# A delta-rule attention and a top-1 router on one core: another order for the attention pipeline, and list scatters that don't wait for each other

## The chip, the cores and the metric

One core of a Trainium2 chip. The time is that of one execution on the device, in microseconds (us). Three runs of the kernel before are known, with a median of 893.73 us (889.64 to 895.54).

## The reference

Two blocks follow each other, all in float32.

```
# attention: 4 batches x 8 heads, 768 tokens, head size 48
k_n = k / (|k| + 1e-6)
for t in range(768):
    y[t]   = q[t] @ state                       # state: 48 x 48 per batch and head, zero at first
    v_old  = k_n[t] @ state
    state += beta[t] * outer(k_n[t], v[t] - v_old)
# the heads side by side: x has 3072 tokens of 384
# router: 8 experts, top 1
logits = (x / |x|) @ (emb / |emb|).T / tau
e      = argmax(logits);  gate = softmax(logits)[e]
out    = gate * (relu(x @ w1[e]) @ w2[e])       # w1: 384 x 1024, w2: 1024 x 384 per expert
```

## The kernel before, in words

**Attention.** Tokens are taken in 12 chunks of 64; a pair of batches stands on the two halves of the 128 partitions (`P2` = 2 such pairs, index `p`; `g` is the half). In a chunk the recurrence is solved in closed form with the inverse of a 64x64 triangular matrix per batch and head. The matrices come from `products` (keys against keys and queries, line 259, masked by `later` on VectorE, line 263). Their 32x32 diagonal blocks for two chunks (a pair `s`) travel through memory: `blocks_out` writes them, `blocks_in` reads them with one block on each partition, `weigh` (GpSimd, line 282) multiplies by beta, `eliminate` (VectorE, lines 290 and 292) inverts them in 31 steps of two operations, `inverses_back` sends them to memory and back, `turn` transposes them, and `lower1` and `lower2` (lines 316 and 326) make the full inverse `W`.

For chunk `c`, `residual` takes the state's part from the values (line 337, subtraction on VectorE in line 348), `solve` applies `W` (line 357), `update` and `keep` bring the state forward with `kl` (unit keys made once more on GpSimd, line 237, from a second load of the keys, `Kl`), and `outputs` makes the chunk's result. `store` writes it to memory as `x`; `turned` and `logits` (line 419) make the router's logits with the transposed tokens as weights and 8 columns. `route` runs after every fourth chunk, three times: it finds the expert and gate of 512 tokens, counts their places (a prefix over 8 columns of tokens, lines 470 and 471) and scatters token numbers into the list `idmap` with eight transfers (line 482).

The order is written out by hand in one loop over `c` from -6 to 11. Iteration `c` works on chunk `c`, makes `W` for `c+1` (`cl`), transposes and products for `c+5` (`cf`), key norms and unit keys for `c+6` (`cn`), and some elimination steps in between (`steps(n)`) and operations of `route` (`fill(n)`). Each engine and each queue takes its instructions in this order. All loads, `Kl` among them, are issued by SyncE; `blocks_out` stands behind the loads of K, Kl and V of the same iteration. All scatters are issued by GpSimd, which waits for one to land before it issues the next.

**Experts.** When all tokens are listed, the lists are cut into 31 tiles of 128 tokens of one expert. For each tile SyncE reads its list (line 632) and both weight matrices (lines 638 and 640), GpSimd gathers the tokens, TensorE transposes them and does both products (lines 654 and 659), and GpSimd scatters the result.

Of the kernel before, what the change touches and what calls it, by code (L numbers as in the profile page):

```python
# [15 lines left out]
C = 64  # L16
# [5 lines left out]
def kernel(  # L22
# [11 lines left out]
):  # L34

# [60 lines left out]
    for g in range(2):  # L96
        nc.gpsimd.iota(tokid[64 * g:64 * g + 64], pattern=[[C, NC], [2 * S, P2]], base=g * S, channel_multiplier=1)
    run = cpool.tile([128, E], F32, name="run")
# [12 lines left out]
    for i in range(P2):  # L111
        Qs.append(ac.tile([128, NP, 2, 64], F32, name=f"Qp{i}"))
        nc.gpsimd.memset(Qs[i], 0.0)
        KNs.append(ac.tile([128, NP, 2, 64], F32, name=f"KN{i}"))
        nc.gpsimd.memset(KNs[i], 0.0)

    def heads(t):

        return t.rearrange("p (a b) d -> p b a d", a=2)

    def load(src, c, name, bufs):
        ts = []
        for p in range(P2):
            t = wk.tile([128, H, D], F32, name=name, tag=name, bufs=bufs)
            for g in range(2):
                nc.sync.dma_start(out=t[64 * g:64 * g + 64],
                                  in_=src[2 * p + g, :, c * C:(c + 1) * C, :].rearrange("h t d -> t h d"))
            ts.append(t)
        return ts

    def load_q(c):
        for p in range(P2):
            for g in range(2):
                for hh in range(2):
                    nc.sync.dma_start(out=Qs[p][64 * g:64 * g + 64, :, hh, 0:D],
                                      in_=q[2 * p + g, hh * NP:(hh + 1) * NP, c * C:(c + 1) * C, :]
                                      .rearrange("h t d -> t h d"))
# [3 lines left out]
    Kf = {0: load(k, 0, "K", 4)}  # L141
    load_q(0)
    Kf[1] = load(k, 1, "K", 4)
# [10 lines left out]


    rtau = ac.tile([128, 1], F32, name="rtau")
    nc.scalar.dma_start(out=rtau, in_=moe_tau.broadcast_to([128, 1]))
    nc.vector.reciprocal(rtau, rtau)
    enT = ac.tile([128, KC, E], F32, name="enT")
    emb = wk.tile([128, Dm], F32, name="emb", tag="R")[0:E]  # L160
    nc.scalar.dma_start(out=emb, in_=moe_expert_emb)
    esq = wk.tile([128, Dm], F32, name="esq", tag="R")[0:E]
    ess = ac.tile([E, 1], F32, name="ess")
    nc.scalar.activation(esq, emb, ACT.Square, accum_out=ess)
    nc.gpsimd.tensor_tensor(out=ess, in0=ess, in1=half[0:E, 0:1], op=ALU.pow)
    nc.vector.tensor_scalar_add(ess, ess, 1e-6)
    nc.vector.reciprocal(ess, ess)
    nc.vector.tensor_scalar_mul(esq, emb, ess)
    psE = bank("f", 3)[:, 0:KC * E].rearrange("p (a e) -> p a e", e=E)
    for j in range(KC):  # L170
        nc.tensor.transpose(psE[:, j, :], esq[:, j * 128:(j + 1) * 128], ident[0:E, 0:E])
    nc.vector.tensor_copy(enT, psE)


    none = ac.tile([128, NMAP // 128], I32, name="none")
    nc.gpsimd.iota(none, pattern=[[0, NMAP // 128]], base=N, channel_multiplier=0)
    nc.scalar.dma_start(idmap.rearrange("(p n) o -> p (n o)", p=128), none)
    zrow = ac.tile([1, Dm + 1], F32, name="zrow")
    nc.vector.memset(zrow, 0.0)
    nc.scalar.dma_start(x_dram[N:N + 1, :], zrow)  # L180
# [17 lines left out]
    for i in range(4):  # L198
        Sb.append(ac.tile([128, 2, NP, 2, D], F32, name=f"S{i}"))
        nc.gpsimd.memset(Sb[i], 0.0)  # L200
# [3 lines left out]
    rns, KQs, APs, kls, Ws, Bks, Tks, Tds, Wds, xcs, Zs = ({} for _ in range(11))  # L204
# [3 lines left out]
    def squares(c):  # L208
# [3 lines left out]
        for p in range(P2):  # L212
            Ksq = wk.tile([128, H, D], F32, name="Ksq", tag="Ksq")
            nc.gpsimd.tensor_tensor(Ksq, Kf[c][p], Kf[c][p], op=ALU.mult)
# [488 lines left out]
```

## Time and profile before

| | |
|---|---|
| median of three runs | 893.73 us |
| the profiled execution | 899.38 us, of which the span of instructions is 897.7 us |
| granted TensorE clock, mean of the span | 0.809 of full speed |
| TensorE products busy | 640.2 us (71% of the span) |
| VectorE, ScalarE, GpSimd busy | 268.5, 158.7 and 212.8 us |

The profile is that of one execution. A granted clock of 1.00 is 2.4 GHz, 0.50 is 1.2 GHz; there are these two levels, and a mean lies between them. A line's number is that of the kernel above. The busy time of an engine says little by itself: TensorE's in the experts' part is not changed by what the attention does. What sets the time of a stretch is the wait that ends last in it.

### The profile page before, as it was taken

The numbers are of one execution on the slowest core, as the hardware profiler recorded it, in microseconds if no ns is written. First come the engines' busy times: TensorE is split into PE (matmuls) and PEld (weight loads), VectorE is DVE, ScalarE is ACT, GpSimd is POOL, SyncE is SP. The second block draws the span as 40 slices with busy tenths as digits, with TensorE's granted clock in tenths as the row PEclk, the third lists the DMA queues.
The fourth block names the chain that finished last, engine by engine and source line by source line (L and its number), as shares of the span: only waits on it lengthen the run. The fifth ranks groups of instructions, "written<-read, shape, count | busy, mean of one in ns | idle before, by whom it ended". The sixth has DMA issues, their size and how long they took to land.

```text
span 897.7 us, 18377 instructions
## 1 busy us (share of the span) xinstructions
PE 640.2 (71%) x7748; PEld 543.3 (61%) x7748; DVE 268.5 (30%) x713; ACT 158.7 (18%) x316; POOL 212.8 (24%) x214
## 2 busy tenths in 40 slices
PE   0525373895829059979763019999999999999995
PEld 0424373894828048878763017777777777777773
DVE  2419674672843036783004000000000000000000
ACT  0211041342312013432321001111111111111110
POOL 4734433223320241110221211211211111111110
PEclk9955577786665557965777559999999999999998
DMA  3343747536443014533030059999999999999930
GB/s 63 67 87 60 137 88 151 88 73 134 89 83 67 8 33 80 116 77 67 2 73 18 0 209 383 380 311 306 324 296 332 300 318 319 301 316 312 312 124 0
DMA packets 216020, 146.00 MB, mean 163 GB/s; under 512 B 164890, under 2 KB 199873, under 8 KB 215938
## 3 DMA queue, kind: packets, MB, share of 16 engines
q1 hardware_dynamic: 210000, 133.75, 52.8%
q0 software_dynamic: 4736, 10.85, 4.0%
q8 instruction: 61, 1.00, 0.5%
q10 hardware_dynamic: 1202, 0.23, 0.1%
q14 instruction: 21, 0.17, 0.1%
HBM read 128.92 MB, written 17.25 MB: 163 GB/s over the span
## 4 chain that ended last, share of the span: by engine, by line
PE 50%; issue 16%; DVE 14%; DMA 12%; POOL 5%; SPq 1%; ACT 1%; POOLq 0%; DVEq 0%
PE psH L654 17%; PE psO L659 16%; DMA idmap<-tokid,slot_i 9%; DVE tmp L290 4%; DVE Tk L292 3%; PE f L326 3%; PE f L246 3%; PE r L357 2%; DVE AP L263 2%; PE f L419 2%; PE r L337 2%; PE f L259 1%; DVE xTm L648 1%; PE f L316 1%; DMA Kl<-in_k_dram 1%
## 5 line engine op out<-in xcount | busy, mean ns | idle before, releaser
L654 PEld LDWEIGHTS psH<-xTm,w 128*128 128x128 f32 x1488 | 170.9, 193 | 18.7 <-DVE xTm L648 14.5
L654 PE MATMUL psH<-xTm,w 128*128 128x128 f32 x1488 | 174.4, 277 | 10.8 <-DVE xTm L648 10.3
L659 PE MATMUL psO<-w,hT 128*128 128x384 f32 x496 | 165.1, 486 | 0.0
L659 PEld LDWEIGHTS psO<-w,hT 128*128 128x128 f32 x496 | 91.9, 190 | 57.5
L661 DVE TENSOR_SCALAR y<-psO,xg 128x384 f32<-128x384 f32 x31 | 19.2, 618 | 319.9 <-PE psO L659 319.9
L656 ACT ACTIVATE hT<-psH 128x512 f32<-128x512 f32 x62 | 37.0, 597 | 363.2 <-PE psH L654 306.3
L290 DVE TENSOR_TENSOR tmp<-Bk,Tk 128x31 f32<-128x31 f32 (+15 forms) x186 | 74.5, 401 | 7.4 <-POOL Bk L282 2.5
L357 PE MATMUL r<-R,W 64*64 64x48 f32 x704 | 30.5, 251 | 60.6 <-DVE R L348 60.4
L634 POOL DMA_INDIRECT xg<-x_dram,ids x31 | 30.1, 971 | 183.1 <-DMA ids<-idmap 109.8
L292 DVE TENSOR_TENSOR Tk<-Tk,tmp 128x31 f32<-128x31 f32 (+15 forms) x186 | 68.5, 368 | 6.4
L357 PEld LDWEIGHTS r<-R,W 64*64 64x64 f32 x704 | 28.3, 167 | 64.6 <-DVE R L348 60.5
L662 POOL DMA_INDIRECT out_dram<-y,ids x31 | 31.3, 1009 | 124.0 <-DVE y L661 121.2
L259 PE MATMUL f<-KQ 48*64 48x128 f32 x768 | 37.1, 325 | 32.0 <-DVE AP L263 32.0
L482 POOL DMA_INDIRECT idmap<-tokid,slot_i x24 | 23.5, 978 | 136.8 <-DMA idmap<-tokid,slot_i 76.2
L259 PEld LDWEIGHTS f<-KQ 48*64 48x64 f32 x768 | 29.9, 165 | 35.5 <-DVE AP L263 33.4
L337 PE MATMUL r<-S,KQ 128*64 128x96 f32 x704 | 48.5, 302 | 0.7 <-issue 0.7
L647 PE MATMUL psX<-ident,xg 128*128 128x128 f32 x93 | 13.5, 278 | 49.4 <-DMA xg<-x_dram,ids 49.4
L326 PE MATMUL f<-Wd,PI 64*64 64x32 f32 x768 | 36.6, 264 | 16.6 <-ACT PI L318 16.5
L326 PEld LDWEIGHTS f<-Wd,PI 64*64 64x64 f32 x768 | 35.1, 189 | 19.6 <-ACT PI L318 18.9
L647 PEld LDWEIGHTS psX<-ident,xg 128*128 128x128 f32 x93 | 11.4, 143 | 54.9 <-issue 52.6
L247 ACT ACTIVATE KQ<-f 128x512 f32<-128x512 f32 x48 | 28.3, 597 | 90.8 <-PE f L246 90.3
L337 PEld LDWEIGHTS r<-S,KQ 128*64 128x64 f32 x704 | 41.0, 174 | 3.2 <-issue 1.9
(123 smaller groups left out, 653.1 us busy)
## 6 DMA issues: line engine op xcount, KB each, us to landing
w<-in_moe_w_dram SPq DMA_DIRECT2D x62, 1536.0 KB
K<-in_k_dram SPq DMA_DIRECT2D x48, 96.0 KB
Qp<-in_q_dram SPq DMA_DIRECT2D x96, 48.0 KB
Kl<-in_k_dram SPq DMA_DIRECT2D x48, 96.0 KB
V<-in_v_dram SPq DMA_DIRECT2D x48, 96.0 KB
x_dram<-xc SPq DMA_DIRECT2D x24, 192.0 KB
a_dram<-AP SPq DMA_DIRECT2D x48, 64.0 KB
Bk<-a_dram SPq DMA_DIRECT2D x6, 512.0 KB
```

The costliest lines, as they stand in the source:

```text
L247: nc.scalar.activation(KQs[c, p][:, :, :, i, :], psT.rearrange("p a (g t) -> p a g t", g=2), ACT.Copy)
L259: nc.tensor.matmul(psG[hh][64 * g:64 * g + 64, 128 * hp:128 * hp + 128], lhsT=KQ[r, hp, g, 0, :], rhs=KQ[r, hp, g, :, :], start=True, stop ...
L290: nc.vector.tensor_tensor(tv, Bk[:, i, i + 1:Q].unsqueeze(2).broadcast_to(sh), Tk[:, i:i + 1, 0:i + 1].broadcast_to(sh), op=ALU.mult)
L292: nc.vector.tensor_tensor(Tk[:, i + 1:Q, 0:i + 1], Tk[:, i + 1:Q, 0:i + 1], tv, op=ALU.subtract)
L326: nc.tensor.matmul(psW[r, m, :], lhsT=PI[r, m, :], rhs=Wds[s][r, n + m, :], start=True, stop=True, skip_group_check=True)
L337: nc.tensor.matmul(ps1[64 * g:64 * g + 64, 2 * D * hp:2 * D * (hp + 1)], lhsT=KQs[c, p][:, hp, g, i, :], rhs=state(c, p)[:, g, hp].rearran ...
L357: nc.tensor.matmul(psZ[r, h, :], lhsT=Ws[c][r, p * H + h, :], rhs=R[r, h, :], start=True, stop=True, skip_group_check=True)
L634: nc.gpsimd.indirect_dma_start(out=x, out_offset=None, in_=x_dram[:, :], in_offset=bass.IndirectOffsetOnAxis(ap=ids[:, 0:1], axis=0))
L654: nc.tensor.matmul(psH[:, i], lhsT=w1[:, j, (f + i) * 128:(f + i + 1) * 128], rhs=xT[:, j, :], start=(j == 0), stop=(j == KC - 1))
L656: nc.scalar.activation(hT[:, f:f + 4, :], psH, ACT.Relu)
L659: nc.tensor.matmul(psO, lhsT=hT[:, f, :], rhs=w2[:, f, :], start=(f == 0), stop=(f == NF - 1))
L662: put = nc.gpsimd.indirect_dma_start(out=out[:, :], out_offset=bass.IndirectOffsetOnAxis(ap=ids[:, 0:1], axis=0), in_=y, in_offset=None, b ...
```

## The change

- **Own prologue.** The loop starts at -5. Ahead of it, the norms and unit keys of chunks 0 and 1 are made with VectorE in GpSimd's place, chunk 0 is transposed, and the router's embeddings, the fill of the list and the zero row move into a function `embeddings` that is called behind this. The first zero fills go from GpSimd to VectorE, and the keys of chunk 1 are loaded on ScalarE's queue.
- **Early products.** In an iteration the two `products` stand between residuals, solves and update, and `blocks_out` right behind them. Key products are masked by VectorE as before; query products are copied by ScalarE and masked by GpSimd (`causal`), in tiles of their own.
- **Late transposes.** Those of chunk `c+6` stand at the end of iteration `c`, between `lower1`, `outputs`, `turned` and `lower2`, which are cut into halves by batch pair.
- **Four array quarters.** `residuals` has 48x64 weights for each head in place of 96 wide pairs of heads (twice as many products), and the outputs of the second pair change halves of the partitions. The `f` accumulators get four banks, `r` two.
- **Transposed logits.** The embeddings, padded to 32, become the weights; the result is copied and transposed back, one iteration later.
- **Spread transfers.** A chunk's queries come in four transfers in place of eight; Q, K and V are issued at the start of an iteration, `Kl` by ScalarE's queue behind `keep`.
- **Unchained scatters.** The eight scatters of a round are declared independent, with a one-element fill between them; each list read waits for all scatters. The prefix over tokens is done by nine products, not by sixteen operations.

```diff
-    Kf = {0: load(k, 0, "K", 4)}
+    Kf = {0: load(k, 0, "K", 4), 1: load(k, 1, "K", 4, nc.scalar)}
     load_q(0)
-    Kf[1] = load(k, 1, "K", 4)
...
+            nc.vector.tensor_tensor(As[c][:, p, hh:H:2], G[:, :, 0], later.broadcast_to([128, NP, C]), op=ALU.mult)
+            nc.scalar.activation(Ps[c][:, p, hh:H:2], G[:, :, 1], ACT.Copy)
+
+    def causal(c, p):
+        nc.gpsimd.tensor_tensor(Ps[c][:, p], Ps[c][:, p], later.broadcast_to([128, H, C]), op=ALU.mult)
...
+    def residuals(c):
         if c == 0:
+            return Vl[c]
+        psK = [bank("r", 2), bank("r", 2)]
+        for p in range(P2):
+            for hp in range(NP):
+                for g in range(2):
+                    for hh in range(2):
+                        r = slice(64 * hh, 64 * hh + D)
+                        o = (p * NP + hp) * D
+                        nc.tensor.matmul(psK[hh][64 * g:64 * g + 64, o:o + D], lhsT=KQs[c, p][r, hp, g, 0, :],
+                                         rhs=state(c, p)[r, g, hp, hh, :], start=True, stop=True,
...
     def logits(c, xTs):
+        psL = bank("f", 4)
+        for i in range(KC):
+            for p in range(P2):
+                nc.tensor.matmul(psL[Q * p:Q * p + Q, 0:128], lhsT=enT[:, i, :], rhs=xTs[p][:, i, :],
+                                 start=(i == 0), stop=(i == KC - 1), skip_group_check=True)
+        lT = wk.tile([P2 * Q, 128], F32, name="lT", tag="lT", bufs=1)
+        nc.scalar.activation(lT, psL[0:P2 * Q, 0:128], ACT.Copy)
...
-        for i, w in enumerate((mask_su, ones)):
-            nc.tensor.matmul(psR[:, i], lhsT=w, rhs=ohf, start=True, stop=True, skip_group_check=True)
+        for j in range(J):
+            nc.tensor.matmul(psR[:, (j + 1) * E:], lhsT=ones, rhs=ohf[:, 0:(J - j) * E],
+                             start=(j == 0), stop=False, skip_group_check=True)
+        nc.tensor.matmul(psR[:, 0:J * E], lhsT=mask_su, rhs=ohf, start=False, stop=True, skip_group_check=True)
...
         for j in range(J):
-            nc.gpsimd.indirect_dma_start(
+            put = nc.gpsimd.indirect_dma_start(
                 out=idmap[:, :], out_offset=bass.IndirectOffsetOnAxis(ap=slot_i[:, j:j + 1], axis=0),
+                in_=tokid[:, b * RC + j // P2, j % P2:j % P2 + 1], in_offset=None).ins
+            tc.declare_no_dep(put, group="places", reason="each token has a place of its own")
+            tc.add_to_no_dep_group("places", put)
+            puts.append(put)
+            nc.gpsimd.memset(between, 0.0)
...
-    for c in range(-6, NC):
+    for c in range(2):
+        sq = squares(c, nc.vector)
+        for p in both:
+            sums(c, p, sq)
+        root(c)
+    inverse_norms(0)
+    unit_keys(0, nc.vector)
+    for p in both:
+        for i in range(2):
+            transposes(0, p, i)
+    load_q(1)
+    Kf[2] = load(k, 2, "K", 4)
+    inverse_norms(1)
+    unit_keys(1, nc.vector)
+    embeddings()
+    for c in range(-5, NC + 1):
```

One iteration after the change, with the conditions at its ends left out (`back` is the pair whose inverses come back, in odd iterations):

```
inverses_back(back); load_q(cn); load K(cn+1); load V(cl)          # SyncE
Rs = residuals(c); squares(cn), sums(cn, 0); unit_keys_again(c, 0..1)
products(cf, 0); solve(c, 0); sums(cn, 1); root(cn); logits(c - 1); solve(c, 1); steps(1)
products(cf, 1); blocks_out(cf); by_token_again(c - 1)
update(c, 0..1); keep(c, 0..1); load Kl(cl)                         # Kl: ScalarE's queue
steps(2); inverse_norms(cn); unit_keys(cn); causal(cf, 0..1)
if cf is odd: blocks_in, diagonal, weigh
steps(4); fill(5); outputs(c, 0); turn(back); transposes(cn, 0, 0); lower1(cl, 0)
steps(2); fill(3); outputs(c, 1); transposes(cn, 0, 1); known(cl); lower1(cl, 1)
steps(2); fill(3); turned(c, 0); store(c); transposes(cn, 1, 0); lower2(cl, 0)
turned(c, 1); transposes(cn, 1, 1); lower2(cl, 1); squared(c, 0..1)
steps(4 if odd else 20); fill(4)
```

## Rows read from the trace of the kernel before

**Rows 1.** The page's chain of waits, by line: shares of the span.

```profile
PE psH L654 17%; PE psO L659 16%; DMA idmap<-tokid,slot_i 9%; DVE tmp L290 4%; DVE Tk L292 3%; PE f L326 3%; PE f L246 3%; PE r L357 2%; DVE AP L263 2%; PE f L419 2%; PE r L337 2%; PE f L259 1%; DVE xTm L648 1%; PE f L316 1%; DMA Kl<-in_k_dram 1%
```

**Rows 2.** Stretches: start, chunk loop, experts (columns: length, busy us, granted clock, DMA).

```profile
core 0: us, PE busy (x) PEld busy (x) DVE busy (x) ACT busy (x) POOL busy (x), PEclk, DMA share, GB/s
0.00:123.80 123.80, 45.49 (x545) 39.23 (x545) 65.77 (x162) 16.93 (x28) 58.80 (x65) 0.70 0.47 87
123.80:479.50 355.70, 250.68 (x5125) 231.46 (x5124) 158.92 (x435) 104.55 (x225) 83.17 (x79) 0.71 0.38 74
...
524.30:897.70 373.40, 342.97 (x2077) 271.66 (x2077) 33.65 (x62) 37.01 (x62) 61.38 (x62) 0.97 0.86 291
```

**Rows 3.** Stretches: two chunks in a row, a slow chunk, the one behind it.

```profile
155.40:215.50 60.10, 46.58 (x964) 43.05 (x964) 35.06 (x86) 20.00 (x42) 19.32 (x18) 0.76 0.52 101
325.20:354.20 29.00, 26.81 (x483) 24.67 (x484) 20.06 (x50) 9.46 (x20) 7.98 (x8) 0.68 0.44 83
354.20:371.30 17.10, 17.06 (x471) 15.70 (x470) 11.06 (x31) 8.87 (x19) 0.00 (x0) 1.00 0.26 59
```

**Rows 4.** Timeline of TensorE in the last two of those stretches.

```profile
348.53 2.83 PE L337 MATMUL r<-S,KQ 128*64 128x96 f32 x32
...
355.26 0.66 PE L246 MATMUL f<-ident,Qp 128*128 128x128 f32 x4
...
356.81 1.06 PE L259 MATMUL f<-KQ 48*64 48x128 f32 x30
...
368.28 1.50 PE L419 MATMUL f<-enT,xT 128*128 128x8 f32 x12
369.72 1.54 PE L337 MATMUL r<-S,KQ 128*64 128x96 f32 x32
```

**Rows 5.** Line 482 by itself: time from a scatter's issue to its landing.

```profile
DMA to landing us min/median/max: 3.0/4.0/4.9
```

**Rows 6.** Timeline of GpSimd: scatters of two rounds (start, us, idle before).

```profile
287.80 1.21 POOL L482 DMA_INDIRECT idmap<-tokid,slot_i  x1 [20.96 <-DVE slot_i L479]
...
322.55 1.61 POOL L214 TENSOR_TENSOR Ksq<-K 128x384 f32<-128x384 f32 x2
...
489.94 1.06 POOL L482 DMA_INDIRECT idmap<-tokid,slot_i  x1 [8.74 <-DVE ends L610]
```

**Rows 7.** Timeline: K's loads and the blocks on SyncE's queue, line 282.

```profile
193.53 2.66 SPq L126 DMA_DIRECT2D K<-in_k_dram  x4
...
202.85 2.20 SPq L271 DMA_DIRECT2D a_dram<-AP  x4
...
210.50 2.34 POOL L282 TENSOR_TENSOR Bk<-Bk,bb 128x1024 f32<-128x1024 f32 x1 [15.00 <-DMA Bk<-a_dram]
```

**Rows 8.** Groups by line (count, busy us, mean ns, idle before).

```profile
L290 DVE TENSOR_TENSOR tmp<-Bk,Tk 128x31 f32<-128x31 f32 (+15 forms) x186 | 74.5, 401 | 7.4 <-POOL Bk L282 2.5
L263 DVE TENSOR_TENSOR AP<-f,later 128x512 f32<-128x512 f32 x48 | 30.3, 673 | 32.0 <-PE f L259 32.0
L292 DVE TENSOR_TENSOR Tk<-Tk,tmp 128x31 f32<-128x31 f32 (+15 forms) x186 | 68.5, 368 | 6.4
L282 POOL TENSOR_TENSOR Bk<-Bk,bb 128x1024 f32<-128x1024 f32 x6 | 14.0, 2339 | 90.9 <-DMA Bk<-a_dram 90.9
```

**Rows 9.** Timeline of the tail: the first two prefix operations of the last round.

```profile
485.08 0.17 DVE L470 TENSOR_TENSOR rk<-rk,run 128x8 f32<-128x8 f32 x1
485.28 0.17 DVE L471 TENSOR_TENSOR run<-run,rk 128x8 f32<-128x8 f32 x1
```

**Rows 10.** Timeline of the start: first transposes, first elimination step, first solve.

```profile
28.78 1.11 PE L246 MATMUL f<-ident,KN 128*128 128x128 f32 x4 [7.65 <-POOL KN L229]
...
64.07 0.18 DVE L290 TENSOR_TENSOR tmp<-Bk,Tk 128x31 f32<-128x31 f32 x1
...
123.78 1.87 PE L357 MATMUL r<-V,W 64*64 64x48 f32 x32
```

**Rows 11.** Timeline of VectorE: the same shape beside GpSimd, and alone.

```profile
166.69 0.96 DVE L290 TENSOR_TENSOR tmp<-Bk,Tk 128x175 f32<-128x175 f32 x1
...
195.76 0.34 DVE L290 TENSOR_TENSOR tmp<-Bk,Tk 128x175 f32<-128x175 f32 x1
```

More of the change, by code (lines that the diff above doesn't have):

```diff
@@ L365, in update @@
                 for hh in range(2):
[L366 removed]
+                    h = 2 * hp + hh
                     r = slice(64 * g, 64 * g + 64)
@@ L525 @@
-        if has(c):
-            Rs = [residual(c, p) for p in both]
+        back = (c + 1) // 2 if odd and 0 <= (c + 1) // 2 < NS else None
+        if back is not None:
+            inverses_back(back)
+        if cn >= 2 and has(cn):
+            load_q(cn)
+        if has(cn + 1) and cn + 1 > 2:
+            Kf[cn + 1] = load(k, cn + 1, "K", 4)
+        if has(cl) and c >= -1:
+            Vl[cl] = load(v, cl, "V", 4)
+        if odd and 0 <= (c + 3) // 2 < NS:
+            elim = eliminate((c + 3) // 2)
@@ L527 @@
+        if has(c):
+            Rs = residuals(c)
+        if cn >= 2 and has(cn):
+            sq = squares(cn)
+            sums(cn, 0, sq)
+        if has(c):
+            for p in both:
+                unit_keys_again(c, p)
         if has(cf):
-            transposes(cf, 0, 0)
-            transposes(cf, 0, 1)
-            transposes(cf, 1, 0)
-        steps(3)
+            products(cf, 0)
         if has(c):
             solve(c, 0, Rs[0])
-        if has(cf):
-            transposes(cf, 1, 1)
+        if cn >= 2 and has(cn):
+            sums(cn, 1, sq)
+            root(cn)
@@ L536 @@
+        if has(c - 1):
+            Lp = logits(c - 1, xTs)
         if has(c):
             solve(c, 1, Rs[1])
+        steps(1)
         if has(cf):
[L539 to L548 removed]
+            products(cf, 1)
+            blocks_out(cf)
@@ L549 @@
+        if has(c - 1):
+            by_token_again(c - 1, *Lp)
+            if (c - 1) % RC == RC - 1:
+                behind.append(route((c - 1) // RC))
         if has(c) and c < NC - 1:
@@ L580 @@
                 squared(c, p)
-            logits(c, xTs)
-            fill(20)
-            if c % RC == RC - 1:
-                behind.append(route(c // RC))
+        steps(4 if odd else 20)
+        fill(4)
     fill(1000)
@@ L632, in fetch @@
         got = nc.sync.dma_start(ids, idmap[bass.ds(s, T), :]).ins
+        for put in puts:
+            tc.add_manual_dep(got, put.name, mybir.DependencyInfo(mybir.DependencyClass.Sync, mybir.DependencyReason.DATA),
+                              reason="all tokens are in their places")
         x = mk.tile([128, Dm + 1], F32, name="xg", tag="xg", bufs=4)
```

323 lines of the change are left out of this document (157 added, 166 removed).

## The prediction

> **What bounds the kernel now.** I read the chain of waits first, then the stretches, then the queues. In the chain the experts' products (lines 654 and 659) hold a third of the span, and the list scatters of line 482 a further 9% [rows 1]: 24 transfers of 128 numbers each, which no engine computes. The stretches cut the span into four [rows 2]: a start of 123.8 us to the first chunk's solve, a chunk loop of 355.7 us (12 chunks, 29.6 us each), a routing tail of 44.8 us between that row's end and the next row's begin, and the experts' 373.4 us with TensorE 92% busy at a granted clock of 0.97. The change leaves the experts' code alone apart from a wait ahead of the first list read, so all is decided in the first 524.3 us. There TensorE is busy for 250.7 us of the loop at clock 0.71, and that clock is the second thing to see. A stretch whose granted clock is 1.00 (2.4 GHz) holds 471 matrix products in 17.1 us with TensorE never idle; the one just before it, nearly as full with 483, took 29.0 us at 0.68 [rows 3]. One line's 32 products took 1.54 us in the one and 2.83 us in the other [rows 4]. So a loop stall costs its length and then slow products behind it. The queues say where the stalls come from. GpSimd issues eight scatters per routing round, each waiting for the one before to land, 3.0 to 4.9 us [rows 5]; in the first round it is held from 287.8 until line 214 at 322.55 [rows 6], and TensorE with it. GpSimd also sits 15 us before line 282, six times and 90.9 us in all [rows 7, 8]: the 32x32 blocks leave only when SyncE has issued K, Kl and V loads, from 193.5 to 202.85, and come back at 210.5.
>
> **Scatters.** The wait between scatters goes. A scatter's instruction is 0.96 to 1.2 us long [rows 6], the added one-element fill is short; I take 1.07 us per scatter, 8 x 1.07 + 4.0 for the last landing = 12.5 us in place of 34.3 us (489.94 to 524.3). If the queue takes them no faster than one landing, nothing is gained; if the issue costs nothing, 30 us is. I take 12.5, since 0.96 us is what the instruction itself shows. In the two earlier rounds GpSimd is held 8.6 us instead of 35, and the next chunk's keys (line 237) and squares stand behind it. The list read now waits for all 24 scatters; behind it on SyncE wait the first two tiles' weights, as before.
>
> **Rest of the tail.** Sixteen prefix operations (0.17 us each, 0.20 from start to start [rows 9]) become two: -3.0 us. Eighteen products with 128-column weights stand in for four: at 0.125 to 0.23 us each (line 419, 12 in 1.50 us [rows 4], and nearly double that when slow) this is +1.7 to +3.2 us, I take 2. The transposed logits add a copy, a transpose and a copy, +1 us. So the 10.4 us from the last logits to the first scatter stay. Tail 10.4 + 12.5 = 22.9, against 44.8: **-21.9**.
>
> **Start.** The first transposes stood at 28.78 us, the first elimination step at 64.07, the first solve at 123.78 [rows 10]. The own prologue squares on VectorE, splits the first K loads over two queues, drops one iteration and moves the router's embeddings behind the first transposes. I put the transposes at 17 us. The embeddings then stand ahead of chunk 0's products on TensorE (transposes), ScalarE and VectorE, and eat some of it: elimination at 48.5, that is -15.5. From there to the solve 59.7 us become 51.5, of which the 31 steps themselves are 31 x (0.401 + 0.368) = 23.8 us [rows 8] and stay. First solve at 100: **-24**. Bounds: -8, if the embeddings' transfers hold everything, and -33.
>
> **A full chunk.** The warm stretch is a whole chunk but for 12 of its 16 transposes: 17.1 + 12 x 0.165 = 19.1 us of TensorE [rows 3, 4]. "Four quarters" turns 32 residual products of 0.048 us into 64 of some 0.035 us (line 259, which has four quarters already: 30 in 1.06): +0.7. The logits with 32 weight columns drop from 1.50 us to about 0.6. TensorE floor: 18.9 us, if its clock stays up. VectorE: 35.1 us busy in a pair of chunks [rows 3]; line 263's eight passes of 0.673 us become eight of half the size (0.34 to 0.67; I take 0.36), so 32.5, or 16.3 us per chunk, with issue gaps of 0.03 us some 17.7. Here GpSimd matters. A multiply of line 290 on 175 elements took 0.34 us by itself and 0.96 us while GpSimd worked [rows 11]. The change adds two masks per chunk there, 2 x 1.17 us by half of line 282's 2.34 us [rows 8]. I add 2 to 3 us: VectorE 20 us. The two engines wait for each other at the residuals (behind the last elimination steps of the chunk before), at the new keys and at the turn of the inverses; I give 3.5 us: **23.5 us** per full chunk, bounds 19.5 and 30 (the present pair's 60.1 / 2).
>
> The Trainium skill's page "SBUF — State Buffer", section "SBUF: two separate sides", calls the port pair of VectorE and GpSimd "an exclusive lock, not a bandwidth split", which speaks against the added masks. The trace agrees as to sign, 0.96 against 0.34 us; what it would make of the time is a rival below.
>
> **What covers the rest.** The blocks now leave after the early products with three, not four, groups of loads ahead of them, and those issued at the chunk's start; line 282's result is needed a chunk later, so its wait lies beside TensorE's outputs and transposes. If that cover fails, 15 us per pair come back. Kl's four issues move to ScalarE, 2.66 us by SyncE's row for four [rows 7], where the output evictions queue behind them, and so do four half-size copies of query products per chunk (1.4 to 2.7 us by line 263's 0.673); ScalarE has 105 us of work in 356 [rows 2], 8.7 per chunk, so both cost nothing unless a chunk runs under 15 us. The late transposes fill the gap in which TensorE waited for the inverses. What is late next is VectorE.
>
> The page "DMA: Bandwidth & Descriptors", section "Rules for kernel authors", of the Trainium skill holds that spreading transfers over queues "only saves sequencer issue time". Here that time is what stands ahead of the blocks, so by the rule, too, the 9 us of issue are worth having, and no landing gets shorter.
>
> **Light chunks.** From the eighth on, products and transposes are gone: 17.1 - 64 x 0.035 - 0.7 = 14 us of TensorE, and the two residual and solve round trips have less beside them. I take 19, 18, 17, 16 and 12 us, 82 in all. The routing rounds add 13: in the first, the power of line 429 queues behind line 282 on GpSimd and VectorE waits for it (about 6), and both rounds hold the next keys 3 to 4 us. Loop: 7 x 23.5 + 82 + 13 = 259.5 us: **-96**.
>
> **Sum.** 100 + 259.5 + 22.9 + 373.4 = 755.8 us of span, and 1.7 us around it: 757.5 us against the profiled 899.38. That execution lies 5.6 us above the median of 893.73, so I take as much off: **752 us**.
>
> **Rivals.** *VectorE or a slow clock keeps the old pace* (18%): the stalls go, but full chunks run at 29 us and light ones at 19.5, since waits for VectorE let the clock fall as at 325 us. Loop 7 x 29 + 97.5 + 13 = 313.5, time 806. For: the present pair keeps 29 to 30 us even in the chunk without the 15 us wait, with TensorE 92% busy at 0.68. Against: its idle part was the turn, which now has transposes beside it.
> *VectorE stands still while GpSimd computes* (12%): three pairs of key operations of 1.6 us each [rows 6], two masks of 1.17 and half of line 282, 8.4 us per chunk, come on top of 17.7: full chunks of 26.1 us, 770. That is the rule of "SBUF — State Buffer" in the Trainium skill taken whole. For: the 0.96 us. Against: VectorE's mean of 0.40 us on line 290 has such meetings in it [rows 8].
> *All fits* (8%): full chunks of 20, light ones of 14.5: loop 225, time 718. For: the 17.1 us stretch. Against: VectorE's 20 us.
> *The scatters stay chained* (4%), by the queue itself or an order kept elsewhere: 22 us at the end and some 26 in the loop return: 800. For: no two scatters overlap in the trace. Against: the wait shown is for the landing.
> *Slower* (2%): kl and the square root for the same chunk stand on GpSimd behind line 282 and the scatters. If each chunk waits w for it, and the clock stays at 1.2 GHz, TensorE's work is 1.84 times as long (2.83 / 1.54): 7 x 34.8 + 5 x 25.8 = 373 us, plus 12w. Start and tail give 45.9, so it decides from w = 3.1 us on (373 + 12w > 355.7 + 45.9 + 9); with 8 us it is 961. Against: GpSimd's own work, 83 us in the loop [rows 2], leaves it half idle even with the masks.
>
> **Numbers.** The forecast has 56% and by itself spans 725 to 782 (full chunk 20.5 to 26, start -12 to -30). With the lock, the chained case and most of the old-pace case, and a little of the fast one, 722 to 812 leaves out about 2 in 10. About 1% is what a measurement can tell from no change; faster by more than that: 0.96, within: 0.02, slower: 0.02.
>
> **What would show it.** Line 482's eight scatters 1.0 to 1.1 us apart; no TensorE idle of over 3 us in the loop; first solve near 100 us; stretches of full chunks at clock 0.9 or more and 22 to 25 us long; the wait of line 282 still there, but no TensorE wait behind it. It is wrong if VectorE waits long for GpSimd's keys or masks, or if the experts' stretch is not 373 us.

## The result, and the profile after

The changed kernel takes 832.23 us (median of four runs, 829.93 to 833.08) against 893.29 us for the kernel before on the same chip: a ratio of 0.9316, 95% interval 0.9279 to 0.9353. Forecast were 752 us, with a range of 722 to 812. The sign was right; of 141 us of gain 61 came. The profiled execution took 832.31 us (span 830.6), so it lies on its median; the 5.6 us taken off in the forecast's last step have no counterpart here.

Here are the stretches of the changed kernel (columns as in [rows 2]): start, chunk loop, tail, experts.

```profile
0.00:109.60 109.60, 44.81 (x579) 40.44 (x581) 73.65 (x175) 25.04 (x52) 58.04 (x59) 0.67 0.49 92
109.60:419.70 310.10, 236.94 (x5485) 210.53 (x5479) 162.37 (x429) 119.38 (x285) 109.02 (x111) 0.76 0.50 88
419.70:453.10 33.40, 4.35 (x19) 4.05 (x19) 7.81 (x40) 0.31 (x2) 10.10 (x17) 0.55 0.03 4
453.10:830.60 377.50, 344.29 (x2077) 272.72 (x2077) 33.63 (x62) 37.02 (x62) 61.38 (x62) 0.97 0.85 288
```

Against the forecast's 100, 259.5, 22.9 and 373.4 us the misses are +9.6, +50.6, +10.5 and +4.1. They sum to 74.8 us, and with the 5.6 to the 80 us by which the median lies higher. Two thirds lie in the loop, and the next view says where in it. It is four stretches from a chunk's solve to the next one's: a plain full chunk, the first routing round, a plain light chunk, the second round.

```profile
187.90:210.30 22.40, 17.72 (x522) 15.76 (x515) 19.36 (x44) 11.58 (x28) 11.05 (x9) 0.95 0.57 109
210.30:271.70 61.40, 30.91 (x533) 26.82 (x535) 21.09 (x66) 12.14 (x29) 24.52 (x29) 0.61 0.55 63
314.80:333.10 18.30, 14.18 (x435) 12.64 (x436) 14.53 (x37) 8.42 (x20) 7.44 (x6) 0.95 0.69 146
333.10:377.20 44.10, 26.54 (x453) 23.30 (x454) 15.45 (x57) 8.62 (x21) 10.15 (x18) 0.62 0.43 43
```

The six full chunks without routing last 25.1, 24.9, 28.2, 22.4, 22.1 and 20.9 us, 23.9 in the mean; forecast were 23.5. The last four last 18.3, 17.5, 15.2 and 9.8; their forecasts were 19, 17, 16 and 12. So the chunk's working held in the mean, with single full chunks between 20.9 and 28.2. The two routing rounds last 61.4 and 44.1 us in place of 23.5 and 18: 64 us on top, where the forecast gave 13. Not all of that is standing still: TensorE is busy 30.91 and 26.54 us in the rounds against 17.72 and 14.18 in the plain chunks, for nearly as many products: the granted clock is 0.61 and 0.62 there and 0.95 in the plain ones.

The timeline of TensorE in the first round (start, us, and in brackets idle time before and its releaser) shows two separate losses.

```profile
220.90 1.12 PE L296 MATMUL f<-Td,A 32*64 32x32 f32 x32
238.47 3.55 PE L450 MATMUL f<-oh,ones 128*128 128x64 f32 x16 [16.46 <-DVE den L454]
...
251.64 0.33 PE L306 MATMUL f<-Wd,PI 64*64 64x32 f32 x3 [1.13 <-issue]
252.40 0.19 PE L306 MATMUL f<-Wd,PI 64*64 64x32 f32 x1 [0.43 <-issue]
253.13 0.28 PE L306 MATMUL f<-Wd,PI 64*64 64x32 f32 x1 [0.55 <-issue]
...
268.82 1.45 PE L323 MATMUL r<-S,KQ 48*64 48x48 f32 x44 [6.24 <-issue]
```

**The order.** TensorE stands 16.5 us before the new counting products (line 450), which the program puts between a chunk's two outputs. GpSimd and VectorE show why: the power of line 422 stands behind line 259, which waits for the blocks, and VectorE's chain of small operations waits for that power. The blocks in turn leave on SyncE's queue only at 223.58 us, behind the loads of K and V that it issues from 214.80 on.

```profile
230.75 2.34 POOL L259 TENSOR_TENSOR Bk<-Bk,bb 128x1024 f32<-128x1024 f32 x1 [5.55 <-DMA Bk<-a_dram]
233.05 1.64 POOL L422 TENSOR_TENSOR ssx<-ssx,half 128x8 f32<-128x8 f32 x1
```

```profile
234.72 0.17 DVE L424 TENSOR_SCALAR ssx<-ssx 128x8 f32<-128x8 f32 x1 [9.19 <-POOL ssx L422]
```

**The traffic.** From 249 us TensorE goes forward in ones and threes, waiting for nothing that the profile can name ("issue"), then stands 6.24 us. GpSimd issues the eight scatters from 245.5 us on (first and last of the round). SyncE's queue has the inverses' write and read in a plain chunk (first two lines) and in this one.

```profile
245.50 1.33 POOL L477 DMA_INDIRECT idmap<-tokid,slot_i  x1 [10.81 <-DVE tmp L267]
...
254.71 0.95 POOL L477 DMA_INDIRECT idmap<-tokid,slot_i  x1 [0.22 <-issue]
```

```profile
180.54 0.34 SPq L274 DMA_DIRECT2D t_dram<-Tk  x1
183.97 3.25 SPq L276 DMA_DIRECT2D Td<-t_dram  x4
...
247.90 0.44 SPq L274 DMA_DIRECT2D t_dram<-Tk  x1
256.42 5.99 SPq L276 DMA_DIRECT2D Td<-t_dram  x4
```

The inverses need 8.5 us from their write to the start of the read, 3.4 in the plain chunk. The last round has the scatters with nothing beside them: GpSimd's first and last, and the first read of the list on SyncE's queue.

```profile
429.99 1.06 POOL L477 DMA_INDIRECT idmap<-tokid,slot_i  x1 [8.66 <-DVE ends L677]
...
438.94 0.96 POOL L477 DMA_INDIRECT idmap<-tokid,slot_i  x1 [0.21 <-issue]
```

```profile
453.14 0.38 SPq L699 DMA_DIRECT2D ids<-idmap  x1
```

They are issued 1.26 us apart (1.37 between the first two) and the list is read 14.2 us after the last: 23.15 us in all, 2.9 per scatter, where [rows 5] had 4.0 each in a chain. The chain of waits agrees: the scatters' share is down from 9% [rows 1] to 2%, not to nothing.

```profile
PE psH L724 18%; PE psO L729 17%; DVE Tk L269 5%; DVE tmp L267 5%; PE r L340 4%; PE f L306 3%; PE f L231 3%; PE f L217 2%; DMA idmap<-tokid,slot_i 2%; PE f L296 1%; DMA ids<-idmap 1%; ACTq L149 1%; PE f L404 1%; PE f L450 1%; PE r L323 1%
```

### The profile page after: what moved, and what is told of

It reads as the page before. It is cut to its first block, busy times and chain, and to the rows that moved or that the text cites. A ratio compares the mean times of both kernels' runs of the same rounds, so it can differ in the third digit from the quotient of the medians.

```text
span 830.6 us, 19239 instructions
## 1 busy us (share of the span) xinstructions
PE 630.4 (76%) x8154; PEld 527.7 (64%) x8154; DVE 277.5 (33%) x706; ACT 181.7 (22%) x400; POOL 238.5 (29%) x248
## 3 DMA queue, kind: packets, MB, share of 16 engines
q8 instruction: 64, 1.05, 0.5%
## 4 chain that ended last, share of the span: by engine, by line
PE 55%; DVE 15%; issue 13%; DMA 8%; POOL 4%; SPq 2%; ACTq 2%; ACT 0%; POOLq 0%; DVEq 0%
PE psH L724 18%; PE psO L729 17%; DVE Tk L269 5%; DVE tmp L267 5%; PE r L340 4%; PE f L306 3%; PE f L231 3%; PE f L217 2%; DMA idmap<-tokid,slot_i 2%; PE f L296 1%; DMA ids<-idmap 1%; ACTq L149 1%; PE f L404 1%; PE f L450 1%; PE r L323 1%
## 5 line engine op out<-in xcount | busy, mean ns | idle before, releaser
L724 PE MATMUL psH<-xTm,w 128*128 128x128 f32 x1488 | 175.5, 279 | 12.0 <-DVE xTm L718 11.3
L269 DVE TENSOR_TENSOR Tk<-Tk,tmp 128x31 f32<-128x31 f32 (+15 forms) x186 | 85.7, 461 | 6.4
L267 DVE TENSOR_TENSOR tmp<-Bk,Tk 128x31 f32<-128x31 f32 (+15 forms) x186 | 81.8, 440 | 7.7 <-POOL Bk L259 2.8
L217 PE MATMUL f<-ident,KN 128*128 128x128 f32 x96 | 21.2, 361 | 62.3 <-POOL KN L201 47.9
L217 PEld LDWEIGHTS f<-ident,KN 128*128 128x128 f32 x96 | 15.3, 187 | 64.4 <-POOL KN L201 49.6
L192 POOL TENSOR_TENSOR rn<-rn,half 128x16 f32<-128x16 f32 x12 | 35.5, 2958 | 61.1 <-DVE rn L189 61.1
L340 PE MATMUL r<-R,W 64*64 64x48 f32 x704 | 34.7, 266 | 20.0 <-DVE R L330 20.0
L340 PEld LDWEIGHTS r<-R,W 64*64 64x64 f32 x704 | 32.4, 182 | 24.4 <-issue 21.1
L704 POOL DMA_INDIRECT xg<-x_dram,ids x31 | 30.0, 967 | 48.1 <-issue 25.7
L306 PEld LDWEIGHTS f<-Wd,PI 64*64 64x64 f32 x768 | 32.7, 164 | 16.3 <-issue 14.8
L240 POOL TENSOR_TENSOR P<-P,later 128x512 f32<-128x512 f32 x24 | 32.4, 1364 | 20.8 <-ACT P L237 20.8
L330 DVE TENSOR_TENSOR R<-V,r 128x192 f32<-128x192 f32 x44 | 12.6, 347 | 72.0 <-PE r L323 72.0
```

The source lines that it names most:

```text
L192: nc.gpsimd.tensor_tensor(out=rns[c].rearrange("p a h -> p (a h)"), in0=rns[c].rearrange("p a h -> p (a h)"), in1=half, op=ALU.pow)
L217: nc.tensor.transpose(psT[:, hp], src[:, 2 * hp:2 * hp + 2].rearrange("p a d -> p (a d)"), ident)
L240: nc.gpsimd.tensor_tensor(Ps[c][:, p], Ps[c][:, p], later.broadcast_to([128, H, C]), op=ALU.mult)
L267: nc.vector.tensor_tensor(tv, Bk[:, i, i + 1:Q].unsqueeze(2).broadcast_to(sh), Tk[:, i:i + 1, 0:i + 1].broadcast_to(sh), op=ALU.mult)
L269: nc.vector.tensor_tensor(Tk[:, i + 1:Q, 0:i + 1], Tk[:, i + 1:Q, 0:i + 1], tv, op=ALU.subtract)
L306: nc.tensor.matmul(psW[r, h, :], lhsT=PI[r, p * H + h, :], rhs=Wds[s][r, n + h, :], start=True, stop=True, skip_group_check=True)
```

## The experiments

Each starts from the changed kernel. Theory A blames the scatters' traffic, theory B the order. The cuts of code are shortened, and arithmetic on places is written as one line.

**1. Scatters after the loop.**

```diff
-        for j in range(J): put = nc.gpsimd.indirect_dma_start(...)
+        late.append((b, slot_i))     # all 24 are issued behind the loop
```

> All 24 scatters of the changed kernel are held until the loop is over; nothing else differs. Theory A (traffic): a scatter of 128 four-byte places needs about 2.9 us of the DMA side however it is issued, and what else is in flight then (the inverses' way through DRAM, the instruction streams) is slowed. Then the two routing rounds in the loop lose their ragged stretches of TensorE, about 12 and 8 us, and the loop falls from 310 to about 290; the tail takes 24 x 2.9 = 70 us for its scatters instead of 23, so about 80 instead of 33.4. Sum about 858. Theory B (order): the rounds lose their time only because TensorE stands behind the route's counting matmuls; scatters are harmless and cost 1.27 us each. Then the loop stays at 310 with the ragged stretches in it, and the tail gains 16 x 1.27 = 20: about 853. The stages tell them apart, not the total.

825.83 us, ratio to the kernel before 0.9257 (0.9201 to 0.9312). The loop is 30 us shorter (solve of the last chunk at 379.9 instead of 409.9), and TensorE's fragments are gone: the routing rounds last 50.6 and 29.3 us, 25.6 less together. So much of their surplus of 64 us goes with the scatters. With them goes GpSimd's own time for issuing, 10.2 us in the first round (245.5 to 255.7), which this run does not separate from the traffic; but in the changed kernel GpSimd is through with the next keys at 258.9, and TensorE isn't through with the residuals before 270. The wait before line 450 stays, 18.2 us. The 24 scatters need 54.4 us from the first (391.56) to the read (445.97), 2.3 each: more than their issue, less than A's 2.9. GpSimd issues eleven in a row and then waits for landings three times (4.1, 1.3 and 4.5 us). A holds for the loop, but its price in the tail was too high; B doesn't explain the loop. Both totals, 858 and 853, were too high.

**2. The list's places apart.** Place s goes to row s mod 128, column s div 128 of a 128 x 223 table, so that neighbouring places lie 892 bytes apart; a tile's list is then one column.

```diff
+        col = slot >> 7; slot = 223 * slot - (NMAP - 1) * col      # five small VectorE operations
-        got = nc.sync.dma_start(ids, idmap[bass.ds(s, T), :]).ins
+        got = nc.sync.dma_start(ids, idmap.rearrange("(p n) o -> p (n o)", p=128)[:, bass.ds(s, 1)]).ins
```

> The list of places is laid out so that neighbouring places lie 892 bytes apart instead of 4 (five small VectorE operations a round, about 1 us); as many scatters, as many bytes. Theory A1: the writes are slow because a scatter's 128 places are runs of neighbouring four-byte words, so that many fall on the same few lines. Then a scatter lands soon after its issue: the last round's 23 us from first scatter to the ids becomes about 12.5, the two rounds in the loop lose 8 to 12 us each: about 802. Theory A2: any four-byte write costs this, wherever it goes: same time within 1% of 832, landing unchanged. Theory B (order) also gives no change in the loop.

802.52 us, 0.8961 (0.8917 to 0.9004): A1's 802. The read of the list comes 2.7 us after the last scatter's issue instead of 14.2, and the inverses wait 2.8 us between write and read.

```profile
426.30 0.96 POOL L483 DMA_INDIRECT idmap<-tokid,slot_i  x1 [0.21 <-issue]
```

```profile
429.04 0.38 SPq L705 DMA_DIRECT2D ids<-idmap  x1
```

So it is where the words lie that makes a scatter slow to land, not their number. That the total came to A1's figure is partly luck: the rounds fell only to 54.9 and 38.0 us, 6.5 and 6.1 less where A1 had 8 to 12 each, and the profiled execution took 808.08 us, the longest of the five. TensorE still goes in fragments from 249 to 258 us: of the 25.6 us that go with the scatters in experiment 1, 12.6 go here, and half is left.

**3. The route's place in the order.**

```diff
+        fill(1)                      # the power, ahead of causal and weigh
-        fill(3)                      # (two places between the outputs)
...
-        steps(4 if odd else 20)
-        fill(4)
+        fill(1)                      # counting products, last in the chunk
+        steps(2 if odd else 10)
+        fill(3)
+        steps(2 if odd else 10)
```

> Only the route's place in the order is changed: the power of GpSimd is issued before the chunk's masks and before it waits for the blocks, the counting matmuls stand at the end of TensorE's chunk instead of between the two outputs, and half of the elimination steps stand behind them. Theory B (order): TensorE's waits of 16.5 us (first round) and 5.0 us (second) before the counting matmuls go, and the scatters' stretch is filled with other work: the rounds' chunks fall from 61.4 and 44.1 to about 30 and 25, total about 780. Theory A (traffic): only the wait goes, the scatters then fall in the next chunk and make its transfers late as before: minus 15 to 20, total about 813.

820.95 us, 0.9217 (0.9149 to 0.9284): above both sums, 8 us over A's 813 and 41 over B's 780. The wait before line 450 is gone and the first round's chunk falls from 61.4 to 34.0 us; but the scatters now fall into the next chunk, and that one lasts 36.0, as A had it. TensorE's timeline there, first fragments of a dozen:

```profile
252.70 0.37 PE L372 MATMUL r<-Z,P 64*64 64x48 f32 x5
253.34 0.35 PE L372 MATMUL r<-Z,P 64*64 64x48 f32 x5 [0.27 <-issue]
254.10 0.30 PE L372 MATMUL r<-Z,P 64*64 64x48 f32 x3 [0.41 <-issue]
254.85 0.32 PE L372 MATMUL r<-Z,P 64*64 64x48 f32 x3 [0.44 <-issue]
...
263.19 1.11 PE L217 MATMUL f<-ident,Qp 128*128 128x128 f32 x4
```

**4. Scatters chained again**, by leaving out the lines that free them from one another.

```diff
-            tc.declare_no_dep(put, group="places", reason="each token has a place of its own")
-            tc.add_to_no_dep_group("places", put)
-            puts.append(put)
-            nc.gpsimd.memset(between, 0.0)
```

> The scatters wait for one another again, as in the kernel before; everything else is as in the changed kernel. By the sum of the prediction unchaining is worth 22 us a round: 832 + 66 = about 898. Theory A (traffic): the DMA side takes 2.9 us a scatter either way, so only the difference to 4.0 to 4.3 comes back: tail plus 11, and 0 to 15 us in each round in the loop, where GpSimd is held up for 34 us instead of 11: 843 to 873.

861.06 us, 0.9643 (0.9591 to 0.9695), inside A's range. Unchaining is thus worth 29 us, not 66, and not the 48 by which the prediction's rival with chained scatters lay above its forecast. With one scatter in flight at a time TensorE shows next to no fragments (two waits of "issue", 0.6 us together, from 241 to 298 us); the next chunk is longer instead (49.3 us), since GpSimd is held until 277.9.

**5. Places apart and the new order together** (2 and 3).

> Places 892 bytes apart and the route's new place in the order, together. What each was worth alone (29.7 and 11.3 us) adds up to 791 us if they touch different time. Theory: with the places spread, transfers are no longer slowed, but TensorE still goes forward in fragments for about 9 us while eight scatters are in flight (it did so in the spread kernel alone); the wait of 16.7 us before the counting matmuls goes. Then the rounds' chunks together exceed plain ones by about 33 us instead of 50: about 785. Rival: the fragments also go, since the scatters fall elsewhere: about 768.

773.53 us, 0.8611 (0.8557 to 0.8665). Alone the two edits were worth 29.7 and 11.3 us, together 58.7, nearest to the rival's 768. The rounds last 33.7 and 26.4 us, and this time there are no fragments, though eight scatters are in flight as before. Its stretches:

```profile
0.00:109.20 109.20, 43.76 (x581) 39.48 (x583) 73.71 (x175) 25.09 (x52) 57.74 (x59) 0.71 0.50 92
109.20:373.10 263.90, 231.10 (x5481) 207.05 (x5477) 173.85 (x440) 118.69 (x285) 109.06 (x111) 0.80 0.49 103
373.10:396.00 22.90, 4.34 (x19) 4.05 (x19) 8.12 (x45) 0.31 (x2) 10.10 (x17) 0.57 0.05 7
396.00:772.70 376.70, 344.82 (x2077) 273.27 (x2077) 33.63 (x62) 37.01 (x62) 61.39 (x62) 0.97 0.83 289
```

Loop 263.9 and tail 22.9 us: the forecast's 259.5 and 22.9. What the forecast took for granted in the changed kernel needs these two edits. That the loop comes so near is partly chance: its rounds still cost 18.6 us more than plain chunks where the forecast gave 13.

**6. One scatter at a time**, at four places of the following chunks, in the first two rounds; on top of 5.

```diff
+            if b < NC // RC - 1:
+                drops.append(put); continue     # issued later, one per drip()
```

> As the kernel with both, but the sixteen scatters of the first two rounds are issued one at a time, each waiting for the one before to land, at four places of each chunk's order on GpSimd over the two chunks that follow; the last round's eight stay unchained. Theory: TensorE's fragments need several scatters in flight; with one at a time they go, and the two rounds win some 9 us each over the kernel with both: about 767. Rival: any scatter holds TensorE for its own microsecond: no gain, about 785; or GpSimd's waits for landings (2.7 us each) delay the keys: slower than 785.

777.79 us, 0.8664 (0.8616 to 0.8713): nothing gained on 5, whose fragments were gone already. GpSimd now waits 21.6 us for landings, and one later chunk lasts 26.6 us instead of 19.4.

**7. The masks on VectorE.**

```diff
-        nc.gpsimd.tensor_tensor(Ps[c][:, p], Ps[c][:, p], later...
+        nc.vector.tensor_tensor(Ps[c][:, p], Ps[c][:, p], later...
```

> The changed kernel with the 24 causal masks (two for each of the 12 chunks) on VectorE instead of GpSimd, nothing else. Theory C (VectorE stands while GpSimd computes): each mask on GpSimd (1.36 us) costs VectorE nearly its own length when both have work; on VectorE it costs about 0.7 us. Then the first solve comes about 4 us earlier than 109.6, plain chunks don't get longer, and the total falls to about 825. Rival (VectorE is simply full): 24 x 0.7 = 17 us more on VectorE, some of it on the path: 835 to 845, the first solve not earlier.

831.35 us, 0.9285 (0.9234 to 0.9335), the changed kernel's time; first solve at 109.2. Neither sum came, and the groups say why (count, busy us, mean ns, idle before). In the changed kernel:

```profile
L269 DVE TENSOR_TENSOR Tk<-Tk,tmp 128x31 f32<-128x31 f32 (+15 forms) x186 | 85.7, 461 | 6.4
L267 DVE TENSOR_TENSOR tmp<-Bk,Tk 128x31 f32<-128x31 f32 (+15 forms) x186 | 81.8, 440 | 7.7 <-POOL Bk L259 2.8
```

and with the masks on VectorE:

```profile
L267 DVE TENSOR_TENSOR tmp<-Bk,Tk 128x31 f32<-128x31 f32 (+15 forms) x186 | 77.6, 417 | 6.8 <-POOL Bk L259 2.0
L269 DVE TENSOR_TENSOR Tk<-Tk,tmp 128x31 f32<-128x31 f32 (+15 forms) x186 | 69.6, 374 | 6.4
L240 DVE TENSOR_TENSOR P<-P,later 128x512 f32<-128x512 f32 x24 | 21.1, 922 | 0.0
```

The steps get 20.3 us shorter (167.5 to 147.2), and the masks take 21.1. In the mean of the 24, a mask on GpSimd had cost VectorE what it costs on VectorE itself.

**8, 9 and 12. How far apart?** G tiles of the list interleaved, places 4G bytes apart, with the order of 3.

```diff
+    G = 4            # 16 and 2 in the other runs
+        slot = (slot // (128 * G)) * 128 * G + slot % 128 * G + slot // 128 % G
-        got = nc.sync.dma_start(ids, idmap[bass.ds(s, T), :]).ins
+        got = nc.sync.dma_start(ids, idmap[bass.ds(s, T, step=G), :]).ins
```

> As the kernel with spread places and the new order, but neighbouring places lie 16 bytes apart (four tiles of the list interleaved) instead of 892. Packed at 4 bytes with this order it took 820.95 us, at 892 bytes 773.53; from the last round's first scatter to the list's first read 23 us packed, 11.7 spread. Theory A1 with small pieces (about 64 bytes): runs of four places still share a piece, so the landing lies between: 13 to 18 us, total 778 to 800. Rival (only words that touch each other disturb one another): as good as 892 bytes, 774. Rival (pieces of hundreds of bytes): as slow as packed, 821.

> As the last, with neighbouring places 64 bytes apart (sixteen tiles interleaved). Theory A1 with small pieces: as good as 892 bytes, 774 plus about 1 us for four more small operations a round. Rival (pieces of hundreds of bytes, or the distance itself): between 790 and 821, the last round's landing still over 15 us.

> As the kernels with 16 and 64 bytes between neighbouring places, now with 8 bytes (two tiles of the list interleaved). At 4 bytes this order took 820.95 us and 24.1 us from the last round's first scatter to the first read of the list; at 16, 64 and 892 bytes 773.82, 772.29 and 773.53 us, and 12.6, 11.8 and 11.7 us. Theory W (only words that touch disturb one another): as at 16 bytes, 774 us and about 12 us. Theory P (a scatter's writes within one piece of 16 bytes, or a little more, follow one another): two places a piece, so about half of the loss: landing about 16 to 18 us, total 790 to 800.

| bytes between places | time, us | ratio to the kernel before | first scatter of the last round to the list's read, us |
|---|---|---|---|
| 4 (experiment 3) | 820.95 | 0.9217 (0.9149 to 0.9284) | 24.1 |
| 8 | 794.85 | 0.8901 (0.8831 to 0.8971) | 16.6 |
| 16 | 773.82 | 0.8646 (0.8599 to 0.8694) | 12.6 |
| 64 | 772.29 | 0.8628 (0.8577 to 0.8678) | 11.8 |
| 892 (experiment 5) | 773.53 | 0.8611 (0.8557 to 0.8665) | 11.7 |

At 8 bytes the executions lie far apart: 786.32, 794.85 and 796.37 us, whose median is in the table, and 800.16. The profiled one is the shortest. Its last column, from GpSimd's timeline and SyncE's queue:

```profile
390.85 1.14 POOL L487 DMA_INDIRECT idmap<-tokid,slot_i  x1 [10.08 <-DVE ends L688]
```

```profile
407.45 0.38 SPq L715 DMA_DIRECT2D ids<-idmap  x1
```

Sixteen bytes are enough, so pieces of 64 bytes or more are out. At eight, where no two words touch, 21 to 22 of the 47 us are left, and 4.9 of the 12.4 us in the last column: theory W, the rival that was right at 16, falls, and theory P (pieces of about 16 bytes) fits both figures. What such a piece is, no run shows. The kernel with 64 bytes, 772.29 us, is the best of the study, with 16 and 892 bytes no different from it.

**10. More elimination steps inside the chunk** (on 5).

```diff
-        steps(1) ... steps(2) ... steps(4) ... steps(2) ... steps(2)
+        steps(2) ... steps(3) ... steps(6) ... steps(3) ... steps(3)
```

> The kernel with spread places and new order, with one or two more elimination steps at each of the five inner places of a chunk, so that an even chunk ends with none or few of them ahead of the next chunk's residuals. Theory: TensorE's waits for the residuals (4.2, 4.2, 2.6 and 3.3 us in the even chunks of the changed kernel) go, and nothing else moves: 773.5 minus 8 to 12 = about 764. Rival: the same steps now stand ahead of the masked products inside the odd chunks, which TensorE needs as much: no gain, 770 to 778.

792.78 us, 0.8860 (0.8801 to 0.8918): 19 us slower, against both. The first four chunks last 28.6, 27.4, 29.0 and 27.9 us instead of 25.0, 22.6, 28.3 and 22.6, and ScalarE's waits for VectorE's masked products rise from 33.7 to 47.3 us in the loop. The residuals' wait was not moved away either, 25.7 us against 22.1 in experiment 5.

**11. Weights ahead of the list** (on 5).

```diff
+        nc.sync.dma_start(w1, ...); nc.sync.dma_start(w2, ...)     # now first in fetch(i)
         got = nc.sync.dma_start(ids, ...)
```

> The kernel with spread places and new order, with each expert tile's two weight loads queued before the list read instead of behind it, so that the first tile's 3 MB start while the last scatters land. Theory: the 4.1 us by which the expert part is longer than in the kernel before lie in the first tile (first transposes 11.3 us after the first list read, before 9.8; first products 8.0 us instead of 7.0), and the weights loading beside the gather cause them: minus 3 to 5, about 769. Rival: the gather's own way sets the first tile, no change; or later tiles' lists, now behind the weights' buffers, come too late: slower by 10 or more.

827.65 us, 0.9272 (0.9203 to 0.9341): the rival, and worse than it said. TensorE waits for gathered tokens thirteen times, 74.2 us, where experiment 5 has one such wait, of 24.8 us:

```profile
PE psX L724 <- DMA xg<-x_dram,ids: 74.2, 13, 33.1
```

A list read takes no longer from issue to landing (6.5 us, 6.7 in experiment 5, medians); it is issued later, behind the weights, and GpSimd's gathers wait for it 155.8 us in 20 waits against 14.4 us in two. The 4.1 us in the experts' stretch stay unexplained but for 2.6 of them: first transposes 1.5 us later after the first list read, first products 1.05 us longer.

## Why the prediction was wrong

**Routing rounds: the step that failed.** "The routing rounds add 13" priced the route by who waits for GpSimd's keys. It was 64. Of these, 25.6 us go with the scatters (experiment 1 takes them away); 18.6 us stay in experiment 5 (33.7 and 26.4 against 23.5 and 18), what counting products and VectorE's route cost in a better place; the remaining 20 us are put down to the order. These parts are differences between runs: no run changes the order alone, since in 3 the scatters move with it. The waits before line 450, 16.5 us in the first round and 5.0 in the second, are of the same size as the last part. The forecast saw the power behind the blocks ("about 6"), but let only VectorE wait for it. It didn't ask what stands behind the counting products on TensorE, which takes them in program order: the second output, the transposes and the next chunk.

**Scatters: price from the wrong row.** I took 1.07 us per scatter, from the length of the instruction, between bounds that included "no faster than one landing". It was 2.9 us, nearer to that bound (4.0) than to 1.07; the tail is 10.5 us longer for it. The Trainium skill's page "Perfetto Trace Analysis", section "DMA Instruction — SWDGE (GPSIMD)", says that such an instruction's profiled end is "when the last DSP finishes generating descriptors (T6), not when the DMA engines finish moving the data (T9)". The trace agrees: the last issue is over at 439.9 us, the list is read at 453.14. With the places apart (experiment 5) the first scatter is 11.7 us ahead of the list's read, close to the forecast's 12.5: what it took for granted is that scatters land as fast as they are issued, and packed ones do not. Of the rows known then, only the landing [rows 5] warned of it. And the forecast priced the waits that unchaining removes, not what eight scatters in flight do to others. The rivals that came nearest to 832 had other mechanisms: "VectorE or a slow clock keeps the old pace" (806) had full chunks of 29 us, and they took 23.9; "the scatters stay chained" (800) is refuted by their issue 1.26 us apart, with no wait between them.

**Start.** First solve at 109.6 us instead of 100. The first transposes stand at 14.41 us, earlier than the forecast's 17, but nothing is won by it: ScalarE first issues sixteen loads of beta, from 6.5 to 18.6 us, and the first eviction of a transpose (line 218) stands behind them. The forecast has no term for these loads; no run moves them.

```profile
14.41 1.09 PE L217 MATMUL f<-ident,KN 128*128 128x128 f32 x4 [14.41 <-DVE KN L201]
L149 ACTq DMA_DIRECT2D bb<-in_beta_dram x16: 678/682/1281, 6.5 to 17.9; - x16
```

The first elimination step began at 51.1 us, 2.6 later than forecast, and from there to the solve it took 58.5 us, not 51.5. Up to 88.4 us 61 operations of VectorE's steps take 31.0 us, where 62 of the kernel before took 23.5: these 7.5 us are about the rest of the miss. The reason is that of [rows 11], the same operations being longer beside GpSimd: with the masks on VectorE (experiment 7) the 62 take 26.6 us, though the masks then take up what is won. VectorE meets a mask, then line 259 on GpSimd:

```profile
56.81 1.27 DVE L267 TENSOR_TENSOR tmp<-Bk,Tk 128x156 f32<-128x156 f32 x1
58.11 1.27 DVE L269 TENSOR_TENSOR Tk<-Tk,tmp 128x156 f32<-128x156 f32 x1
...
79.15 2.58 DVE L269 TENSOR_TENSOR Tk<-Tk,tmp 128x220 f32<-128x220 f32 x1
```

The forecast charged that sharing to the full chunk, where it was about right, and took the start's 31 steps as unchanged. *VectorE stands still while GpSimd computes*, the rival at 770 us, thus has its mechanism in the trace: by experiment 7, 24 masks of 1.36 us on GpSimd had lengthened VectorE's steps by 20.3 us, 0.85 each. As a sum for the chunk it was too dear, 23.9 us and not 26.1. The rule of the Trainium skill's page "SBUF — State Buffer", section "SBUF: two separate sides", an exclusive lock on the port pair of VectorE and GpSimd, agrees in sign; 0.85 us is less than the whole 1.36 of a mask.

**What held.** Full chunks at 23.9 us, light ones within 2.2 us of their forecasts; the wait of line 282 (now 259) is 33.9 us in all, 30.5 of it in the loop, instead of 90.9 (7.3 to 31.7 each time, where the prediction read 15 six times), and outside the rounds no TensorE wait stands behind it; Kl's issues on ScalarE's queue cost TensorE nothing: GpSimd waits 41.7 us in the loop for Kl's landing instead of 20.4, but TensorE waits 0.8 us for kl. "No TensorE idle over 3 us" failed at the residuals too (4.3, 4.2 and 3.3 us), behind elimination steps on VectorE; the other places of experiment 10 are worse. **Experts**: 4.1 us longer, see 11.

## What to carry to other kernels

Price an asynchronous transfer by its landing, and ask what else is in flight while it lands; an instruction's own length says only when its engine is free. A piece of work put into an in-order engine's stream costs all that stands behind it until its last input arrives: trace that input back through every queue, and place the piece where the input is already there. Here scattered single words landed at the pace of their issue once neighbouring places lay 16 bytes apart; laying the list out that way cost a handful of small operations a round (five for 892 bytes) and won 30 to 47 us.

## What the runs showed of the hardware

- Scatters of 128 four-byte words, eight in flight: 2.9 us each, from the first issue to the list's read, when neighbouring places touch; at 16 bytes and more they land at the pace of their issue (1.26 us), and the read comes 2.7 to 3.6 us after the last one's.
- Behind packed scatters other transfers slow down: DMA queues in 258 to 264 us of the changed kernel (packets, MB, share of 16 engines' time), 29 GB/s with the engines' time full, and the same queue in the plain stretch from 188 to 206 us (last line). By these shares a packet takes 75 ns there and 15 in the plain stretch. That the scatters are still in flight then is taken from the last round, where the read comes 14.2 us after the last issue; the last one here is issued at 254.71 us, and their own queue has no packet in the window.

```profile
DMA packets 1394, 0.18 MB, mean 29 GB/s; under 512 B 1394, under 2 KB 1394, under 8 KB 1394
...
q1 hardware_dynamic: 1394, 0.18, 109.4%
...
q1 hardware_dynamic: 8309, 1.43, 43.2%
```

  The Trainium skill's page "DMA: Bandwidth & Descriptors", section "Queues, rings and completion order", states that a transfer's semaphore write "lands only after every earlier write from that SDMA engine, across its queues". That fits the inverses' 8.5 us; no run here separates it from slow memory.
- TensorE's fragments are not explained. Instructions come in packets during the run (queue q8, "instruction"): 64 packets for 16308 products and weight loads of TensorE, 255 to a packet, so that the queue is taken to be TensorE's. The plain stretch of 18 us from 188 to 206 has four of them, the stretch from 246 to 264 none; experiment 5 has three in the same stretch and no fragments (first line below). But the packets go with the work: TensorE starts 1028 instructions in the first stretch, 261 in the second and 984 in the third, so a silent queue can be what slow progress looks like. Only one sign speaks for late instructions as a cause: the next packet starts at 264.5 us and takes 3.3 us by its share of the engines' time (second line, 264 to 266 us), where a plain one takes about 1, and TensorE's stand of 6.24 us ends at 268.82, 1 us behind it.

```profile
q8 instruction: 3, 0.05, 1.2%
...
q8 instruction: 1, 0.02, 10.4%
```

  Experiment 2 has fragments too, and its next packet (258 to 260 us) takes 0.9 us. Why its spread places still bring fragments and those of experiment 5 don't is open; beside the former ran the inverses' 1 MB, beside the latter loads and blocks.
- Two edits that touched the same stretch were worth 41 us apart and 59 us together: in 3 the scatters moved into the next chunk and did their harm there.
